# The end of a fused transformer block: score PSUM reopened as single banks, denominators turned by 32x32 transposes, late W1 groups through gelu from PSUM

## Chip, cores, metric

One NeuronCore of a Trainium2 chip. The metric is the device time of one execution, in microseconds (us). The times below are medians of runs in the fast state; no run used here was marked slow, and one (e10_turn_thrice) is a single run of unknown state, used only for its trace. Besides the whole time I use the **tail**: in one trace, the stretch from the end of the last exp (which is the start of the following `ACT_TABLE_LOAD` on ScalarE) to the end of the span. It turns out to repeat far better than the whole time does.

In the views of the profile, PE is TensorE, DVE is VectorE, ACT is ScalarE and POOL is GpSimd. The **granted clock** of a run is the mean share of its full clock that TensorE was given, as the profiler lists it.

## The reference

An adaLN-conditioned block: layer norm, attention with 32 heads of 16 (S = 2048, D = 512), residual, layer norm, a dense layer of 1376 with gelu, residual. All inputs are bf16.

```python
mod = (_silu(c) @ w_mod).reshape(c.shape[0], 6, 1, -1)
sa, ca, ga, sb, cb, gb = (mod[:, i].copy() for i in range(6))
h = _layernorm(x) * (1 + ca) + sa
x = x + ga * _A_ref(h, A_wqkv, A_wo)          # attention
h = _layernorm(x) * (1 + cb) + sb
x = x + gb * _B_ref(h, B_w1, B_b1, B_w2, B_b2)  # gelu(h @ w1 + b1) @ w2 + b2
```

## The kernel before

A small list scheduler inside the kernel places every operation. `op(engine, fn, us, deps, ...)` makes one, `acq=` takes a buffer from a pool (`Res`), `rel=` gives buffers back, and `gate=` holds an operation until a condition is true. TensorE computes scores, ScalarE takes exps of 1536 or 1024 columns from PSUM, VectorE does some of the exps in another way ("shifts"), TensorE multiplies by V with a column of ones (so row 16 of each 32 holds the denominator), and W1, W2 and Wo fill the gaps.

Queries come in four blocks of 512. For the last block all heads of the first 256 queries are done first, so that their dense layer (`block_tail(b, 2)`, here called the **older half**) can partly run under the exps. The last 256 queries are two tiles of 128, **tile 2** and **tile 3** (`last_half`). In the traces a table load of 1.28 us stands between the last exp and the first gelu (`ACT_TABLE_LOAD`), and the kernel holds back all gelus of both halves until the last exp is done.

```python
    SPAN = (3, 2)
    ...
    r_st = [res(f"st{n}", 1, [P, n * QB], FP32, pp) for n in SPAN]   # scores: one tile of 3 banks, one of 2
    r_od = res("od", 1, [P, QB], FP32, pp)                            # P @ V of the current heads
    r_ax = res("ax", 2, [P, QB], FP32, pp)                            # everything else
    ...
    # block_tail, the older half (part = nt < TPB)
        for f in range(NF):                                           # NF = 11 groups of W1
            mm = chain([(lambda ps, f=f, j=j: nc.tensor.matmul(
                out=ps[:, 0:N], lhsT=W1[:, j, f * P:(f + 1) * P], rhs=h.tile[:, j, 0:N],
                start=(j == 0), stop=(j == NC - 1)), nt * MM / NC) for j in range(NC)],
                hd + [o_late["w1"], g], kind, r_ax, (h,))
            ev.append(op("DVE", lambda o, f=f, mm=mm: nc.vector.tensor_scalar(      # add b1, to SBUF
                out=g.tile[:, f, 0:N], in0=mm.tile[:, 0:N], scalar1=b1c[:, f:f + 1], scalar2=None,
                op0=ALU.add), ...))
        if part:                                                      # three gelus in SBUF after the last exp
            ge = [op("ACT", ... Gelu_apprx_tanh ...,
                gate=lambda: units[0] == NR * NT * 4) for lo, hi in ((0, 4), (4, 8), (8, NF))]
    ...
    # last_half: tiles 2 and 3
        big = [take(x) for x in r_st]
        r_t = Res("t", sum(SPAN), lambda i: big[i >= SPAN[0]].tile[       # five slots in the two score tiles
            :, (i % SPAN[0]) * QB:(i % SPAN[0] + 1) * QB])
        acc = {t: take(r_t, big) for t in tiles}
        ...
        for n, t in enumerate(tiles):
            ml = []
            for p in range(2):
                cols = slice(p * HB + (t % 2) * P, p * HB + (t % 2 + 1) * P)
                sh = ... nc.vector.stream_shuffle(out=OD.tile[:, cols], in_=od.tile[:, cols], mask=[16] * 32)
                rc = ... nc.vector.reciprocal(out=OD.tile[:, cols], in_=OD.tile[:, cols])     # 128 columns
                ml.append(... nc.vector.tensor_tensor(out=OT.tile[:, cols], in0=od.tile[:, cols],
                                                      in1=OD.tile[:, cols], op=ALU.mult))
            ...   # 2 Wo matmuls (WoP), y = ps * ga, residual, statistics, rstd on GpSimd, z, 4 PE transposes,
            ...   # 2 modulations on VectorE and 2 on ScalarE
            for f in range(NF):                                       # 4 matmuls of 128 columns, then gelu from PSUM
                mm = op("PE", w1, 4 * 0.071, hd, lat=PEL, mode=full, kind="last", acq=r_t, prio=0.3)
                gd.append(op("ACT", ... Gelu_apprx_tanh, bias=b1c[:, f:f + 1] ..., (mm,), prio=0.3, rel=(mm,)))
            ...   # 12 matmuls of W2 (one is the bias row), y, residual, store
```

The softmax here doesn't subtract the row's maximum and nothing guards it: scores larger than these inputs give would overflow.

## Time and profile before

| | before |
|---|---|
| time, median (range), first 3 runs | 823.44 us (823.07 to 825.82) |
| span of the profiled run | 818.1 us |
| last exp's end | 784.05 us |
| tail | 34.05 us |
| first W1 matmul of tile 2 begins / last one ends, after the last exp's end | 10.5 / 16.1 us |
| last W1 matmul of tile 3 ends, after the last exp's end | 24.7 us |

The prediction below quotes the main lines and says how they are read. Here is one view more: ScalarE's timeline of tile 3 in the kernel before. Columns are start, duration of the row, engine, line, operation, output and input with sizes, count, and in brackets the idle time ahead of the row and what ended it.

```profile
804.00 0.81 ACT L1186 ACTIVATE g<-st,b1c 128x128 bf16<-128x128 f32 x2 [0.30 <-PE st L1183]
805.29 0.88 ACT L1186 ACTIVATE g<-st,b1c 128x128 bf16<-128x128 f32 x3 [0.47 <-PE st L1183]
806.61 0.37 ACT L1186 ACTIVATE g<-st,b1c 128x128 bf16<-128x128 f32 x1 [0.44 <-PE st L1183]
```

ScalarE does one to three gelus and then waits 0.3 to 0.5 us for TensorE. TensorE in turn waits for ScalarE, here in one row of its timeline and then in the summary of waits from 784 us on (engine, line, what it waited for: total us, times, longest):

```profile
804.87 0.61 PE L1183 MATMUL st<-blk,W 128*128 128x128 bf16 x8 [0.46 <-ACT g L1186]
```

```profile
ACT g L1186 <- PE st L1183: 4.1, 10, 0.9
PE st L1183 <- ACT g L1186: 3.7, 8, 1.0
```

### The profile page before, as it was taken

What the parts mean: (1) busy time and instruction counts of PE and PEld (TensorE: products, weight loads), DVE (VectorE), ACT (ScalarE), POOL (GpSimd) and SP (SyncE); (2) the same over time, 40 slices, a digit from 0 to 9 for tenths busy, and PEclk for the clock granted to TensorE, in tenths of its full rate; (3) what the DMA queues carried; (4) which work ended last, traced back from release to release, by engine and by line L of the source; (5) the groups of instructions that cost most, each with busy time, mean ns of one, the idle gap of its engine ahead of it and who ended that gap; (6) DMA issues with size and microseconds to landing.
All of it is one profiled execution on the core that took longest, in us unless ns stands there. A gap on an engine that the chain in (4) does not pass through costs nothing.

```text
span 818.1 us, 20211 instructions
## 1 busy us (share of the span) xinstructions
PE 754.6 (92%) x8236; PEld 281.0 (34%) x8236; DVE 740.1 (90%) x1296; ACT 768.8 (94%) x688; POOL 95.1 (12%) x238
## 2 busy tenths in 40 slices
PE   7889999999989999989999999999999899999996
PEld 3433333332223232222233233232233344434453
DVE  7728997989999999988999999888999999999992
ACT  2899999999999999989999999999999999999963
POOL 4321303100001100000000100000002100010010
PEclk9999999999999999979999999999999999999999
DMA  6304100102100000001100000010100001001110
GB/s 206 104 1 125 27 17 16 30 21 66 41 19 15 18 16 16 18 1 31 48 22 19 15 6 15 24 29 21 45 15 20 11 12 42 18 24 29 24 36 20
DMA packets 34199, 26.22 MB, mean 32 GB/s; under 512 B 15006, under 2 KB 29503, under 8 KB 34107
## 3 DMA queue, kind: packets, MB, share of 16 engines
q1 hardware_dynamic: 33578, 24.94, 10.8%
q8 instruction: 64, 1.05, 0.5%
q14 instruction: 29, 0.23, 0.1%
q10 hardware_dynamic: 528, 0.00, 0.0%
HBM read 21.30 MB, written 2.61 MB: 29 GB/s over the span
## 4 chain that ended last, share of the span: by engine, by line
ACT 39%; PE 28%; DVE 17%; issue 13%; DMA 2%; SPq 0%; ACTq 0%; DVEq 0%
ACT pt L797 37%; PE od L886 9%; PE st L748 8%; DVE ph L838 7%; DVE sh L853 6%; PE ax L1041 2%; PE ax L1072 2%; PE ax L748 2%; ACT g L1085 1%; DMA xb<-in_A_x_dram 1%; PE ax L643 1%; DVE g L1076 1%; DVE OD L911 1%; ACT blk L574 1%; PE st L1183 1%
## 5 line engine op out<-in xcount | busy, mean ns | idle before, releaser
L797 ACT ACTIVATE pt<-st 128x1536 bf16<-128x1536 f32 x635 | 724.3, 1289 | 11.6 <-PE st L748 9.2
L838 DVE TENSOR_SCALAR ph<-ax 128x512 int16<-128x512 f32 x460 | 299.1, 681 | 16.0 <-PE ax L748 13.7
L853 DVE TENSOR_SCALAR sh<-ph 128x2048 int16<-128x2048 int16 x460 | 299.3, 689 | 2.7 <-PE od L886 2.4
L748 PE MATMUL st<-qm,kT 32*128 32x512 bf16 x1588 | 249.8, 385 | 30.0 <-ACT pt L797 23.1
L748 PEld LDWEIGHTS <-kT 32*128 32x128 bf16 x2048 | 86.1, 91 | 257.1 <-issue 246.2
L886 PE MATMUL od<-sh,VX 128*32 128x512 bf16 (+1 forms) x2336 | 163.5, 340 | 5.9 <-DVE sh L853 4.8
L748 PE MATMUL ax<-qm,kT 32*128 32x512 bf16 x460 | 161.9, 382 | 6.6 <-DVE ph L838 4.7
L886 PE MATMUL od<-pt,VEB 128*32 128x512 bf16 (+1 forms) x1976 | 151.6, 343 | 0.9 <-ACT pt L797 0.4
L886 PEld LDWEIGHTS <-VEB 128*32 128x32 bf16 x2560 | 64.9, 96 | 77.2 <-issue 61.5
L886 PEld LDWEIGHTS <-VX 128*32 128x32 bf16 x2336 | 57.9, 95 | 81.9 <-issue 71.7
L938 POOL TENSOR_TENSOR OT<-OD,RB 128x256 bf16<-128x256 f32 x38 | 28.2, 752 | 332.6 <-DVE sh L853 239.3
L886 PE MATMUL od<-ph,VEB 128*32 128x512 bf16 (+1 forms) x584 | 46.6, 341 | 1.5 <-DVE OD L911 1.5
L1072 PE MATMUL ax<-blk,W 128*128 128x512 bf16 (+1 forms) x176 | 41.5, 354 | 0.9 <-DVE ph L838 0.4
L938 POOL TENSOR_TENSOR OS<-OD,RB 128x256 bf16<-128x256 f32 x24 | 17.3, 728 | 205.5 <-DVE sh L853 170.8
L643 PE MATMUL ax<-blk,w 128*128 128x512 bf16 x124 | 36.5, 382 | 2.9 <-ACT blk L574 1.6
L1041 PE MATMUL ax<-w,g 128*128 128x512 bf16 x112 | 31.9, 400 | 0.9 <-ACT g L1085 0.9
L684 POOL TENSOR_SCALAR VX<-VEB 128x128 bf16<-128x128 bf16 x64 | 22.8, 356 | 77.0 <-DVE VEB L584 73.3
L1076 DVE TENSOR_SCALAR g<-ax,b1c 128x512 bf16<-128x512 f32 (+1 forms) x44 | 29.5, 676 | 0.4 <-PE ax L1072 0.2
L911 DVE COPY OD<-od 128x512 f32<-128x512 f32 x31 | 21.1, 681 | 7.4 <-issue 6.3
L558 DVE BATCH_NORM_STATS2 ln_s<-xb 128x6 f32<-128x512 bf16 x32 | 21.6, 675 | 2.4 <-DMA xb<-in_A_x_dram 2.3
L1041 PEld LDWEIGHTS <-g 128*128 128x128 bf16 x176 | 14.4, 99 | 26.9 <-issue 15.0
L584 DVE CAST VEB<-ax 128x512 bf16<-128x512 f32 x15 | 10.2, 681 | 12.8 <-PE ax L668 12.8
(110 smaller groups left out, 382.1 us busy)
## 6 DMA issues: line engine op xcount, KB each, us to landing
RB<-rn SPq DMA_DIRECT2D x124, 64.0 KB
xb<-in_A_x_dram SPq DMA_DIRECT2D x8, 512.0 KB
out_dram<-o SPq DMA_DIRECT2D x16, 128.0 KB
w<-in_A_wqkv_dram SPq DMA_DIRECT2D x3, 512.0 KB
W<-in_B_w_dram SPq DMA_DIRECT2D x1, 1376.0 KB
blk<-in_w_mod_dram SPq DMA_DIRECT2D x2, 512.0 KB
g<-in_w_mod_dram SPq DMA_DIRECT2D x2, 512.0 KB
xb<-in_w_mod_dram SPq DMA_DIRECT2D x2, 512.0 KB
```

Of the source, the lines that this page charges most:

```text
L643: return chain([(lambda ps, j=j: nc.tensor.matmul(out=ps[:, 0:QB], lhsT=w.tile[:, j, cc * P:(cc + 1) * P], rhs=o_h[b].tile[:, j, :], start ...
L684: nc.gpsimd.tensor_scalar(out=v_cols(VX[(t, ph)])[:, 8 * cc:8 * cc + 8, 0:16], in0=v_cols(v_tile(t, 0))[:, 8 * cc:8 * cc + 8, 0:16], scala ...
L748: nc.tensor.matmul(out=o.tile[:, k * QB:(k + 1) * QB], lhsT=kT[cc][kb][rows, ko * P:(ko + 1) * P], rhs=qm.tile[rows, par, :] if hb is None ...
L797: nc.scalar.activation(out=e.tile[:, 0:len(got) * QB], in_=o.tile[:, 0:len(got) * QB], func=ACT.Exp, scale=ESC)
L838: nc.vector.tensor_scalar(out=ph.tile[:, o.row * QB:(o.row + 1) * QB], in0=o.tile, scalar1=PH_B, scalar2=0.0, op0=ALU.add, op1=ALU.max)
L853: sh = op("DVE", lambda o, j=j: nc.vector.tensor_scalar(out=o.tile, in0=first.tile, scalar1=PH_SH[j], scalar2=None, op0=ALU.add), 0.6, es, ...
L886: nc.tensor.matmul(out=o_od[r].tile[32 * i:32 * i + 32, n * HB:n * HB + w], lhsT=v_tile(kt, ph)[:, c0:c0 + 32], rhs=got[i][:, at:at + w], ...
L911: OD = op("DVE", lambda o: nc.vector.tensor_copy(out=o.tile, in_=od.tile), 0.6, (last,), prio=0.0, acq=r_OD, rel=(od,))
L938: two = [op("POOL", lambda o, c=c: after_dve(nc.gpsimd.tensor_tensor(out=OT.tile[:, c * HB:(c + 1) * HB], in0=OD.tile[:, c * HB:(c + 1) * HB],
L1041: nc.tensor.matmul(out=ps, lhsT=g[:, f, col:col + P], rhs=rhs, start=False, stop=(f == NF - 1))
L1072: mm = chain([(lambda ps, f=f, j=j: nc.tensor.matmul(out=ps[:, 0:N], lhsT=W1[:, j, f * P:(f + 1) * P], rhs=h.tile[:, j, 0:N], start=(j == ...
L1076: ev.append(op("DVE", lambda o, f=f, mm=mm: nc.vector.tensor_scalar(out=g.tile[:, f, 0:N], in0=mm.tile[:, 0:N], scalar1=b1c[:, f:f + 1], s ...
```

## The change

The intent is to shorten what follows the last exp, in three parts. **Banks**: the PSUM pool of the scores is closed after the last exp and reopened as five tiles of one bank, so that a wait on one group is no longer a wait on its neighbours. **Turns**: the denominators are brought to eight columns by a 32x32 transpose, divided there, and transposed back, in place of a shuffle and a reciprocal over 128 columns. **Direct**: of the older half, W1 groups 4 to 10 wait for the last exp, go to the new banks, and are read by gelu straight from PSUM, bias included; VectorE's seven adds go.

```diff
+    PSUM_F = 4
-    r_st = [res(f"st{n}", 1, [P, n * QB], FP32, pp) for n in SPAN]
+    scores = ExitStack()
+    ps = scores.enter_context(tc.tile_pool(name="ps", bufs=1, space=psum))
+    r_st = [res(f"st{n}", 1, [P, n * QB], FP32, ps) for n in SPAN]
...
+    def bank(i):
+        if not banks:
+            scores.close()
+            pt = ctx.enter_context(tc.tile_pool(name="pt", bufs=1, space=psum))
+            banks.extend(pt.tile([P, QB], FP32, name=f"t{n}") for n in range(sum(SPAN)))
+        return banks[i]
+    r_t = Res("t", sum(SPAN), bank)
...
         for f in range(NF):
+            direct = part and f >= PSUM_F
             mm = chain([...
-                hd + [o_late["w1"], g], kind, r_ax, (h,))
+                hd + [o_late["w1"], g, over if direct else None], kind,
+                r_t if direct else r_ax, (h,))
+            if direct:
+                ev.append(op("ACT", lambda o, f=f, mm=mm: nc.scalar.activation(
+                    out=g.tile[:, f, 0:N], in_=mm.tile[:, 0:N], func=ACT.Gelu_apprx_tanh,
+                    bias=b1c[:, f:f + 1], scale=1.0), 0.36, (mm,), lat=0.15, prio=0.4, rel=(mm,)))
+                continue
...
-                gate=lambda: units[0] == NR * NT * 4) for lo, hi in ((0, 4), (4, 8), (8, NF))]
+                gate=finished) for lo, hi in ((0, 2), (2, PSUM_F))]
...
-                sh = ... stream_shuffle(out=OD.tile[:, cols], in_=od.tile[:, cols], mask=[16] * 32)
-                rc = ... reciprocal(out=OD.tile[:, cols], in_=OD.tile[:, cols])
-                ml.append(... tensor_tensor(out=OT.tile[:, cols], in0=od.tile[:, cols], in1=OD.tile[:, cols], op=ALU.mult))
+            sh = ... transpose(out=turned(0), in_=half(od.tile))
+            rc = ... reciprocal(out=den, in_=OD.tile[:, 16:HB:32])                       # 8 columns
+            bk = ... transpose(out=turned(1)..., in_=den.unsqueeze(2).to_broadcast([P, 8, 32]))
+            ml = [... tensor_tensor(out=half(OT.tile), in0=half(od.tile), in1=turned(1), op=ALU.mult)]
...
-                    o.ps = big[o.slot >= SPAN[0]].tile.bitcast(BF16)[:, c0:c0 + 2 * P]
+                    o.ps = o.tile.bitcast(BF16)[:, 0:2 * P]
```

More of the change, by code (lines that the diff above doesn't have):

```diff
@@ L1042, in w2_mm, with finished, open_banks, go @@
                              start=False, stop=(f == NF - 1))
+    def finished():
+        return units[0] == NR * NT * 4
+    banks = []
+    def bank(i):
[5 more added lines that the diff above has]
+    r_t = Res("t", sum(SPAN), bank)
+    r_t.free[:] = [1e18] * sum(SPAN)
+    def open_banks():
+        def go(o):
+            for n in range(sum(SPAN)):
+                r_t.free[n] = o.end
+        big = [op("POOL", None, 0.0, (), lat=0.0, prio=0.0, acq=x, gate=finished) for x in r_st]
+        op("POOL", go, 0.0, big, lat=0.0, prio=0.0)
     def block_tail(b, nt=TPB):
@@ L1070, in block_tail @@
         ev = []
+        over = op("POOL", None, 0.0, (), lat=0.0, prio=0.0, gate=finished) if part else None
+        if part:
+            open_banks()
         for f in range(NF):
+            direct = part and f >= PSUM_F
             mm = chain([(lambda ps, f=f, j=j: nc.tensor.matmul(
@@ L1093, in block_tail @@
                         for f in range(NF)], (prev, o_late["w2"]), "part" if part else kind, r_ax, (g,), 3,
-                       lambda f: ge[f // 4 if part else 0])
+                       lambda f: ge[0] if not part else ge[f >= 2] if f < PSUM_F else ev[f])
             prev = mm
@@ L1121, in last_half @@
         tiles = (2, 3)
-        big = [take(x) for x in r_st]
-        r_t = Res("t", sum(SPAN), lambda i: big[i >= SPAN[0]].tile[
-            :, (i % SPAN[0]) * QB:(i % SPAN[0] + 1) * QB])
-        acc = {t: take(r_t, big) for t in tiles}
+        acc = {t: take(r_t) for t in tiles}
         early = {t: op("PE", lambda o, t=t: wo_mm(acc[t].tile, b, t, 0, 3), 3 * MM,
@@ L1130, in last_half, with half, turned @@
         for n, t in enumerate(tiles):
-            ml = []
-            for p in range(2):
-                cols = slice(p * HB + (t % 2) * P, p * HB + (t % 2 + 1) * P)
-                sh = op("DVE", lambda o, cols=cols: nc.vector.stream_shuffle(
-                    out=OD.tile[:, cols], in_=od.tile[:, cols], mask=[16] * 32), 0.25,
-                    (o_last[r], OD, s), prio=0.06 + n)
-                rc = op("DVE", lambda o, cols=cols: nc.vector.reciprocal(
-                    out=OD.tile[:, cols], in_=OD.tile[:, cols]), 0.9, (sh,), prio=0.05 + n)
-                ml.append(op("DVE", lambda o, cols=cols: nc.vector.tensor_tensor(
-                    out=OT.tile[:, cols], in0=od.tile[:, cols], in1=OD.tile[:, cols], op=ALU.mult),
-                    0.25, (rc, OT), prio=0.04 + n))
+            den = work.tile([P, 8], FP32, name=f"den{t}")
+            def half(x, t=t):
+                return x.rearrange("p (a q) -> p a q", a=2)[:, :, (t % 2) * P:(t % 2 + 1) * P]
+            def turned(n):
+                return OD.tile[:, n * HB:(n + 1) * HB].rearrange("p (a q) -> p a q", a=2)
+            sh = op("DVE", lambda o, t=t, half=half: nc.vector.transpose(out=turned(0), in_=half(od.tile)), 0.35,
+                    (o_last[r], OD, s), prio=0.06 + n)
+            rc = op("DVE", lambda o, den=den: nc.vector.reciprocal(
+                out=den, in_=OD.tile[:, 16:HB:32]), 0.12, (sh,), prio=0.05 + n)
+            bk = op("DVE", lambda o, den=den: nc.vector.transpose(
+                out=turned(1).rearrange("p a q -> p (a q)"),
+                in_=den.unsqueeze(2).to_broadcast([P, 8, 32])), 0.35, (rc,), prio=0.045 + n)
+            ml = [op("DVE", lambda o, t=t, half=half: nc.vector.tensor_tensor(
+                out=half(OT.tile), in0=half(od.tile), in1=turned(1), op=ALU.mult),
+                0.36, (bk, OT), prio=0.04 + n)]
             def wo2(o, t=t):
@@ L1167, in tr @@
                 def tr(o, t=t, js=js):
-                    c0 = (o.slot % SPAN[0]) * 2 * QB
-                    o.ps = big[o.slot >= SPAN[0]].tile.bitcast(BF16)[:, c0:c0 + 2 * P]
+                    o.ps = o.tile.bitcast(BF16)[:, 0:2 * P]
                     for n, j in enumerate(js):
```

## The prediction

> **What bounds the kernel now.** I read the page first, then the table of busy time by stretch, then the timeline of each engine and the chain that ended last for the final 40 us, then the waits there. The page says that ScalarE's exps set the pace of nearly the whole span: 635 of them fill 724 us and have 11.6 us of idle time before them.
>
> ```profile
> span 818.1 us, 20211 instructions
> L797 ACT ACTIVATE pt<-st 128x1536 bf16<-128x1536 f32 x635 | 724.3, 1289 | 11.6 <-PE st L748 9.2
> ```
>
> The change leaves that part alone. The built kernels show it: on ScalarE and VectorE the order of instructions is the same up to the last exp and the last of the shifts before the last PV matmuls; on TensorE the first difference is some ten microseconds before that, where two groups of W1 matmuls are taken out. So the question is the tail: from the last exp's end at 784.05 to the span's end at 818.1 lie 34.05 us, and only there can time move. By stretch (columns: length, then busy time and instruction counts of each engine, clock):
>
> ```profile
> 784.00:790.00 6.00, 5.27 (x52) 2.98 (x43) 6.00 (x18) 3.42 (x4) 0.00 (x0) 1.00 0.16 55
> 790.00:795.00 5.00, 4.90 (x28) 2.08 (x28) 4.97 (x16) 1.68 (x4) 0.79 (x2) 1.00 0.00 0
> 795.00:800.00 5.00, 3.15 (x42) 2.53 (x40) 2.84 (x7) 3.09 (x10) 0.80 (x2) 1.00 0.09 30
> 800.00:805.00 5.00, 3.87 (x32) 2.13 (x30) 0.69 (x2) 2.02 (x5) 0.00 (x0) 1.00 0.00 0
> 805.00:810.00 5.00, 3.28 (x37) 2.10 (x36) 0.70 (x2) 2.75 (x9) 0.00 (x0) 1.00 0.00 0
> ```
>
> The tail has two regimes. Up to 795 VectorE is full (6.00 of 6.00, 4.97 of 5.00). From 795 to 810 nobody is: TensorE 10.3 of 15 us, ScalarE 7.9. VectorE's full stretch holds the denominators of the last heads (shuffle, reciprocal, multiply, twice for each token tile) and seven bias adds of W1:
>
> ```profile
> 785.26 0.29 DVE L1134 STREAM_SHUFFLE OD<-od 128x128 f32<-128x128 f32 x1
> 785.46 1.75 DVE L1137 RECIPROCAL OD<-OD 128x128 f32<-128x128 f32 x2
> 787.13 0.41 DVE L1140 TENSOR_TENSOR OT<-od,OD 128x128 bf16<-128x128 f32 x2
> 787.47 0.86 DVE L1076 TENSOR_SCALAR g<-ax,b1c 128x256 bf16<-128x256 f32 x2
> 788.25 0.67 DVE L1151 TENSOR_TENSOR y<-st,ga_bc 128x512 bf16<-128x512 f32 x1
> ```
>
> The later regime is a ping-pong, in the chain that ended last: one or two groups of W1, then gelu, then W1 again; and then a block of W2 that nothing hides.
>
> ```profile
> 805.29 0.63 ACT g L1186 x2
> 805.92 0.04 issue
> 805.96 0.62 PE st L1183 x8
> 806.58 0.02 issue
> 806.61 0.38 ACT g L1186
> 806.98 0.04 issue
> 807.02 0.40 PE st L1183 x4
> ...
> 809.81 2.48 PE st L1041 x11
> 812.29 1.31 PE ax L1041 x6
> ```
>
> Five banks of scores are free by then, but they are two tiles, one of three banks and one of two. A matmul into one bank of a tile waits for the gelu that reads another bank of it: the waits list TensorE's W1 behind gelu for 3.7 us and gelu behind W1 for 4.1 us, and the second tile's PSUM transposes cost the same sort of alternation (802.0 to 803.7, VectorE, ScalarE, VectorE, ScalarE in turn).
>
> [...] The 128x128 f32 shuffle here took 294 ns; a 128x256 transpose is then about 0.43 us (estimate; no transpose on VectorE is in this trace). [...] reciprocal [...] 128x128 took 0.938 us, 128x16 took 0.241, 128x4 took 0.178; 128x8 is about 0.20.
>
> **The change, part by part.** Times below continue the trace of before, so that 784.05 is still the last exp. Paces from rows of the trace: a 512-column matmul every 0.217 us (eight in 1.90, the first 0.38), a 256-column one 0.112, a 128-column one 0.056, each 0.17 more until its result is seen; gelu 128x128 0.367 alone and 0.25 apart in a row, hence 128x256 about 0.47 and 0.36; a hand-over 0.03.
>
> Denominators. Removed on the path for the first tile: the shuffles at 785.04 to the multiplies' end at 787.54, then two bias adds, so that y began at 788.25. Added: the last PV matmul ends near 784.8, transpose 0.43, reciprocal 0.20, transpose 0.43, one multiply over 256 columns 0.41, four hand-overs 0.12: 786.4. TensorE reaches the two Wo matmuls by then (six early Wo 1.3 from 784.7, five W1 of 256 columns 0.56: 786.6), 0.43 and 0.17: y begins at about 787.2, 1.05 us earlier. From y on the durations stay: y 0.69, add 0.42, statistics 0.69 and 0.18, GpSimd 0.97, z 0.41, with hand-overs 3.5: z at 790.7.
>
> W1 from PSUM. Seven bias adds (7 x 0.466 = 3.3 us of VectorE) and three large gelus (1.06, 1.06, 0.84) go; two 128x512 gelus of about 0.62 and seven 128x256 at 0.36 come, 3.6 us on ScalarE in place of 3.0, but beside other work. Seven groups of four 256-column matmuls, two of them formerly under the exps, take TensorE from 786.0 to about 789.6 with the two Wo matmuls. Then eight of the W2 matmuls (0.31 for the bias row and six at 0.217, two more later) fill its time: the transposes start at 791.2, where z no longer holds them; they started at 792.82.
>
> Token tile 2. Transposes 0.23, ScalarE's two modulations end at about 792.4, W1 begins 792.4 (before: 794.55). Now five groups are in flight, so the eleven gelus run 0.25 apart: first at 792.8, last ends 795.7; before, 794.97 to 800.56. Between the modulations TensorE also does the second tile's Wo matmuls, so its y begins near 792.0, where it began at 795.62. That is the largest single step: 3.6 us, of which the old wait in front of those matmuls (OT of tile 3 and the shared score tile) is all.
>
> Token tile 3. The same 3.5 us from y to z: 795.5. W1 of tile 2 is done at 794.9, bias row and one W2 by 795.4, so transposes at 795.5 (before 801.49). Each half now has its own bank: ScalarE done at 796.8 (before 803.71). Eleven gelus on four banks, 0.25 apart: 797.2 to 800.1, TensorE's last W1 at 799.3. Here 9.3 us are won in all, the last W1 matmuls being at 808.6 before and at 799.3 now.
>
> The block at the end. Some is given back. In the built order 20 matmuls of 512 columns followed the last W1 group before (2, 12, 6). Now it is 6, 12, 3 and 12, so 33, because the second W2 group of the older half is put last. Two are bias rows: 31 x 0.217 + 2 x 0.31 = 7.3 us, from 799.3 to 806.6, and 0.17 more. Before, it ended at 813.6. So 2.5 us of the 9.3 go back, 6.8 remain. After that y 0.69, add 0.42 and hand-overs bring 808.0, against 814.77, and the output transfer with the end takes the same 3.3 us. Sum: 811.3 in place of 818.1, 6.8 us less. A second count agrees: all of TensorE's work from 784.7 is 54 matmuls of 512 columns (11.7), four bias rows (1.2), 28 of 256 (3.1) and 96 of 128 (5.4): 21.4 us, to 806.1 if it never waited. It would be all but saturated, so a longer transpose or gelu gains or loses little, and there is nothing more to win without less matmul work.
>
> **The rivals.** First, TensorE's order binds: it takes its queue in order, and one late z or OT stalls everything behind. For it: slacks are only 0.3 to 0.5 us at both transposes. Each of four such points could cost 0.3 to 0.5, and the gain falls to about 5 us: 818.5. Against it: the W2 pieces are placed exactly there. Second, the 32x32 transposes from PSUM, or with a repeated source, run at half the rate: 0.53 us more on the first tile, partly under W1: 817.3. Third, reopening the score banks adds a wait for all exps, or the five banks still depend on each other. Against: in the built kernel each W1 group waits for the one earlier reader of its bank. If it were so, the tail keeps the ping-pong of 9 us and the W2 surplus remains: about 824. Fourth, the whole 34 us are 4% of the span, so even a perfect tail cannot reach 2% (16.5 us): TensorE's 21.4 us stand against it.
>
> **Range and chances.** The worked gain is 6.8 us; I take 6.5, since small hand-overs tend to be missed and not overcounted: 823.44 - 6.5 = 816.9. The low end 815.0 is a gain of 8.4, with W2 a little faster and noise of a run; the high end 819.2 has the first rival in full and 0.7 us of run spread (823.07 to 825.82 before). A change over 2% either way has about one chance in a hundred each.
>
> **What would show it.** Last exp unchanged near 784; transposes of about 0.43 us and a reciprocal of about 0.2; second y 3.5 us earlier; gelus 0.25 us apart in rows of eleven, TensorE's waits on gelu nearly gone; 33 unbroken W2 matmuls of some 7.3 us at the end; TensorE over 95% busy from 785 to 807. Wrong would be: gaps of 0.4 us between gelus, a TensorE wait over 0.5 us at transposes, or a different time of the last exp.

Some of these figures, with what the traces show beside them:

- A transpose of 128x256 at 0.43 us was an estimate of mine: 0.294 us of the 128x128 shuffle and 0.133 us for 128 columns more. VectorE's f32 copies in the trace of before give that for 128 columns (166 ns for 8 columns at L546, 691 and 684 for 512 at L1022: 1.035 ns a column), but no trace then showed that a transpose keeps this pace. The four of the changed kernel took 417 to 452 ns. The second rival's 0.53 us is 512 columns at 1.035 ns more each.
- The reciprocals of 128, 16 and 4 columns, 0.938, 0.241 and 0.178 us, lie 6.2 ns a column apart from 16 to 128 and 5.3 from 4 to 16. Eight columns took 0.204 us in the changed kernel.
- The 128x256 gelu at 0.47 alone and 0.36 apart is an estimate too: in the trace of before gelus of 1024 and 768 columns took 1.057 and 0.843 us, so 0.107 for 128 columns. In the changed kernel one took 0.475 us, and the row of six took 2.66 us, 0.437 apart, near the 0.45 of the four W1 matmuls (0.112 each) that feed one.
- That TensorE takes its queue in order, as the first rival has it, shows in e10_turn_thrice: it stood 0.35 us for z with two matmuls later in its queue whose inputs were ready.

## The result and the profile after

The changed kernel took 815.74 us (median of 4 runs, 811.54 to 818.25), the kernel before 823.26 us in 4 runs. The ratio is 0.990 (95% interval 0.985 to 0.995): "same" by the 2% rule, and inside the predicted range. A ratio here and below is the mean time of one kernel's fast runs over the mean of the other's fast runs of the same rounds, so it is not quite the ratio of the medians.

The page of the changed kernel, in its lines for the span and the exps:

```profile
span 809.7 us, 20210 instructions
L800 ACT ACTIVATE pt<-st 128x1536 bf16<-128x1536 f32 x635 | 723.9, 1286 | 10.1 <-PE st L751 6.7
```

The exps are unchanged. ScalarE's timeline shows where the tail starts and how the gelus of tiles 2 and 3 run now:

```profile
782.08 1.28 ACT L1114 ACT_TABLE_LOAD   x1
...
790.92 2.95 ACT L1222 ACTIVATE g<-t,b1c 128x128 bf16<-128x128 f32 x11 [0.30 <-PE t L1219]
...
795.39 2.95 ACT L1222 ACTIVATE g<-t,b1c 128x128 bf16<-128x128 f32 x11 [0.30 <-PE t L1219]
```

Eleven gelus are one row, (2.95 - 0.37) / 10 = 0.258 us apart. The tail is 809.7 - 782.08 = 27.62 us, 6.43 less than before. The other 1.97 us of this profile's gain lie ahead of the last exp; the experiments show them to be run noise. VectorE, with both y rows that mark when a tile's layer norm can begin:

```profile
783.02 0.45 DVE L1169 STREAM_TRANSPOSE OD<-od 128x256 f32<-128x256 f32 x1 [0.56 <-issue]
783.51 0.20 DVE L1171 RECIPROCAL den<-OD 128x8 f32<-128x8 f32 x1
783.75 0.45 DVE L1173 STREAM_TRANSPOSE OD<-den 128x256 f32<-128x256 f32 x1
784.23 0.42 DVE L1176 TENSOR_TENSOR OT<-od,OD 128x256 bf16<-128x256 f32 x1
...
790.28 0.68 DVE L1188 TENSOR_TENSOR y<-t,ga_bc 128x512 bf16<-128x512 f32 x1
```

And the stretches that answer to those of before (length, then busy time of TensorE, its weight loads, VectorE, ScalarE, GpSimd; last the clock, the DMA share and GB/s):

```profile
782.00:787.00 5.00, 5.00 (x54) 3.40 (x54) 3.41 (x8) 4.30 (x9) 0.00 (x0) 1.00 0.22 74
787.00:792.00 5.00, 5.00 (x50) 3.33 (x48) 4.42 (x12) 3.23 (x11) 0.80 (x2) 1.00 0.00 2
792.00:797.00 5.00, 4.91 (x65) 3.81 (x63) 1.34 (x5) 4.29 (x17) 0.80 (x2) 1.00 0.01 3
797.00:802.00 5.00, 5.00 (x32) 2.45 (x30) 1.17 (x3) 1.34 (x6) 0.00 (x0) 1.00 0.08 26
```

TensorE, which had 10.3 of 15 us between 795 and 810, is now busy in 19.91 of 20 us. All 44 W1 matmuls of a tile are one row of its timeline:

```profile
790.47 2.65 PE L1219 MATMUL t<-blk,W 128*128 128x128 bf16 x44
...
794.94 2.80 PE L1219 MATMUL t<-blk,W 128*128 128x128 bf16 x44
```

The tail ends with W2, from 797.58 to 805.28. "Busy" counts a matmul until its result is seen, so short pauses between matmuls don't show (each of a row of 128-column ones is listed with 0.218 us, and they come 0.057 apart): by the paces of the prediction the same work adds up to 21.4 us, and it took 22.4 (from 782.85 to 805.28).

### The profile page after: what moved, and what is told of

It is laid out like the page before. It is cut to its first block, busy times and chain, and to the rows that moved or that the text cites. A ratio compares the mean times of both kernels' runs of the same rounds, so it can differ in the third digit from the quotient of the medians.

```text
span 809.7 us, 20210 instructions
## 1 busy us (share of the span) xinstructions
PE 751.2 (93%) x8236; PEld 280.0 (35%) x8236; DVE 735.9 (91%) x1281; ACT 768.6 (95%) x694; POOL 95.4 (12%) x238
## 4 chain that ended last, share of the span: by engine, by line
ACT 39%; PE 27%; DVE 16%; issue 14%; DMA 2%; SPq 1%; POOL 0%; POOLq 0%; DVEq 0%; ACTq 0%
ACT pt L800 37%; PE od L889 9%; PE st L751 8%; DVE ph L841 7%; DVE sh L856 6%; PE ax L1044 2%; PE ax L751 2%; PE ax L1100 2%; DMA xb<-in_A_x_dram 1%; PE ax L646 1%; ACT g L1119 1%; DVE g L1110 1%; DVE OD L914 1%; PE t L1044 1%; PE ax L1036 1%
## 5 line engine op out<-in xcount | busy, mean ns | idle before, releaser
L800 ACT ACTIVATE pt<-st 128x1536 bf16<-128x1536 f32 x635 | 723.9, 1286 | 10.1 <-PE st L751 6.7
L751 PE MATMUL st<-qm,kT 32*128 32x512 bf16 x1588 | 250.2, 385 | 29.5 <-ACT pt L800 22.7
L1100 PE MATMUL ax<-blk,W 128*128 128x512 bf16 (+1 forms) x148 | 37.8, 370 | 0.6 <-DVE ph L841 0.4
L1110 DVE TENSOR_SCALAR g<-ax,b1c 128x512 bf16<-128x512 f32 (+1 forms) x37 | 26.5, 719 | 0.4 <-PE ax L1100 0.2
L587 DVE CAST VEB<-ax 128x512 bf16<-128x512 f32 x15 | 10.3, 683 | 12.8 <-PE ax L671 12.8
```

What stands on the lines that cost most here:

```text
L751: nc.tensor.matmul(out=o.tile[:, k * QB:(k + 1) * QB], lhsT=kT[cc][kb][rows, ko * P:(ko + 1) * P], rhs=qm.tile[rows, par, :] if hb is None ...
L800: nc.scalar.activation(out=e.tile[:, 0:len(got) * QB], in_=o.tile[:, 0:len(got) * QB], func=ACT.Exp, scale=ESC)
L1100: mm = chain([(lambda ps, f=f, j=j: nc.tensor.matmul(out=ps[:, 0:N], lhsT=W1[:, j, f * P:(f + 1) * P], rhs=h.tile[:, j, 0:N], start=(j == ...
```

## The experiments

All gave right results. Tails are read from each run's own trace. "Equal clock" is a fit of mine over the 151 fast runs of the jobs below and the first four of the changed kernel: one level for each kernel and one common slope of the span on the run's mean granted TensorE clock (0.969 to 0.992). The slope is -0.42 us for each 0.001 of clock, and the scatter about it 1.2 us (within one kernel and without the slope it is 2.0).

| kernel | time, median | ratio to before (95%) | tail | tail against 34.05 | span at equal clock against before (95%) |
|---|---|---|---|---|---|
| changed (first runs; e6_after) | 815.74; 815.40 | 0.990 (0.985-0.995); 0.990 (0.988-0.993) | 27.62; 27.68 | -6.4 | -6.4 ± 0.8 |
| e1_banks: banks | 815.12 | 0.992 (0.989-0.994) | 27.80 | -6.25 | -5.6 ± 0.8 |
| e2_turns: turns | 821.82 | 1.000 (0.998-1.001) | 34.52 | +0.5 | +0.3 ± 0.7 |
| e3_no_turns: banks, direct | 814.62 | 0.991 (0.988-0.994) | 27.63 | -6.4 | -6.5 ± 0.9 |
| e4_no_direct: banks, turns | 816.45 | 0.994 (0.991-0.996) | 28.57 | -5.5 | -5.2 ± 0.8 |
| e5_before: the kernel before | 822.21 | 1.000 (0.998-1.002) | 34.06 | 0.0 | |
| e7_banks3: three banks | 814.57 | 0.990 (0.987-0.993) | 28.00 | -6.05 | -6.6 ± 1.0 |
| e8_psumf6; e11_psumf6_again | 816.42; 813.96 | 0.991 (0.988-0.994); 0.991 (0.989-0.993) | 26.69; 26.60 | -7.4 | -7.3 ± 0.7 |
| e9_psumf6_no_turns | 814.47 | 0.992 (0.989-0.994) | 26.82 | -7.2 | -7.3 ± 1.0 |
| e10_turn_thrice (one run) | 815.00 | | 28.22 | -5.8 | |

My theory (A) was that the shared score tiles made the ping-pong, and that once it is gone TensorE's total work sets the length of the tail. Its rivals: (B) VectorE, full for the first 11 us, was what held the tail, so denominators and bias adds carry the gain; (C) three parts of about equal worth.

### e1_banks: the five banks alone

```diff
 (changed kernel)
-            direct = part and f >= PSUM_F
+            direct = False          # and the three SBUF gelus, the shuffle and the long reciprocal of before
```

> The five one-bank score tiles alone; denominators by shuffle and reciprocal and the seven bias adds on VectorE as before. Measure: the tail, from the end of the last exp to the end of the span (34.05 us before, 27.62 after). Theory A (the shared score tiles made the ping-pong; once that is gone TensorE's work sets the end): tile 2 starts as before, but its eleven gelus run 0.25 us apart, the Wo matmuls of tile 3 no longer wait behind them, z of tile 3 comes near 15 us after the last exp, and only 20 W2 matmuls follow the last W1: tail 27.4 to 28.4, nearly the whole gain. Theory B (VectorE, full until 795, was what held the tail, so denominators and bias adds carry the gain): at most 3 us are won, tail 31 or more. Theory C (three parts of about 2 us each): tail near 32.

Tail 27.80, as A says: 6.25 of the 6.43 us come from the storage of five PSUM groups alone. In its ScalarE timeline:

```profile
785.50 1.28 ACT L1114 ACT_TABLE_LOAD   x1
...
801.98 2.94 ACT L1216 ACTIVATE g<-t,b1c 128x128 bf16<-128x128 f32 x11 [0.31 <-PE t L1213]
```

The eleven gelus of tile 3 are one row, though denominators and bias adds are those of before. But y of tile 3 starts at

```profile
796.87 0.69 DVE L1182 TENSOR_TENSOR y<-t,ga_bc 128x512 bf16<-128x512 f32 x1
```

which is 11.37 us after the last exp's end. Before it was 11.57, in the changed kernel it is 8.20. So the banks hardly move that y, and still win the tail. The rows of TensorE's timeline come in the same order as in the kernel before, a few missing records aside; what the banks took away is waiting. In the first 20 us after the last exp TensorE is busy for 18.86 us, against 16.65 before; the transposes of tile 3 start 14.94 us after the last exp's end in place of 17.44, and its W1 is done at 18.7 in place of 24.5.

This tail isn't yet full, though: TensorE has 0.9 us less to do here than in the changed kernel (two W1 groups run under the exps), and stands twice near the start, 0.35 us for the denominators and 0.34 us for a bias add.

### e2_turns: the transposes alone

```diff
 (kernel before)
-            shuffle, reciprocal over 128 columns, multiply, twice a tile
+            transpose, reciprocal over 8 columns, transpose, multiply
```

> The 32x32 transposes alone, on the two old score tiles. Theory A: y of tile 2 comes about 0.8 us earlier and the second Wo matmuls 1.5 to 2 us earlier, but the gelu ping-pong of tiles 2 and 3 stays, and the scheduler now leaves 30 W2 matmuls for after the last W1 where it left 20: tail 33.5 to 34.8, no gain. Theory B: tail 31 or less. Theory C: tail near 32.

Tail 34.52: no gain, a half microsecond lost, as A says. The y of tile 3 begins 9.96 us after the last exp's end, 1.6 us earlier than before, and the time goes again: TensorE still stops for readers of the shared tile, once for y itself:

```profile
796.79 0.83 PE L1189 MATMUL st<-blk,W 128*128 128x128 bf16 x12 [0.78 <-DVE y L1157]
```

and 30 matmuls of W2 remain after the last W1 where 20 did (by the built order; 29 of the 30 are in the trace). B and C fall with e1 and e2.

### e3_no_turns: the changed kernel with the old denominators

```diff
 (changed kernel)
-            transpose, reciprocal over 8 columns, transpose, multiply
+            shuffle, reciprocal over 128 columns, multiply, twice a tile
```

> The changed kernel with the old denominators (banks and late gelu from PSUM stay). Theory A: TensorE is so nearly full that W2 and W1 matmuls fill the time in which VectorE divides; tail 27.3 to 28.3, within 0.7 us of the changed kernel. Theory B: the reciprocals (3.6 us of VectorE) come back onto the path, tail 29.5 or more. Theory C: tail near 29.7.

Tail 27.63 against 27.62: nothing lost. The y of tile 3 is again at 11.37 us after the last exp's end, 3.2 us later than in the changed kernel, and it doesn't matter. While VectorE divides, TensorE does W1 and W2 of the older half; what it has done by then it need not do at the end (18 matmuls of W2 after the last W1, where the changed kernel has 33).

### e4_no_direct: the changed kernel with the old bias adds

```diff
 (changed kernel)
-            direct = part and f >= PSUM_F
+            direct = False          # and the three SBUF gelus of before
```

> The changed kernel with the old bias adds on VectorE and three gelus in SBUF (banks and transposes stay). Two W1 groups (0.9 us of TensorE) then run under the exps again. Theory A: tail 26.8 to 27.7, the same as or a little shorter than the changed kernel, since TensorE has 0.9 us less to do there while VectorE's adds lie beside it. Theory B: 3.3 us of bias adds come back onto VectorE, tail 29 or more. Theory C: tail near 29.7.

Tail 28.57, 0.95 us longer than the changed kernel and outside what A expected; B and C expected more still. The TensorE timeline shows what I missed:

```profile
791.42 1.32 PE L1100 MATMUL ax<-blk,W 128*128 128x256 bf16 x8 [0.70 <-DVE g L1110]
793.33 0.37 PE L1041 MATMUL ax<-b_row,ones_row 1*128 1x512 bf16 x1 [0.59 <-DVE g L1110]
```

On the two `ax` tiles, W1 of the older half goes at the pace of VectorE's adds, some of which queue between y, residual and statistics of tile 2: four of the seven come after y, where in e1_banks three do. TensorE stands 1.3 us for them (in e1_banks 0.34 for an add and 0.35 for the denominators), more than the 0.9 us of work that it has less. So the direct gelus are worth about 0.95 us beside banks and turns, but only 0.17 us beside banks alone (27.80 to 27.63), where the scheduler put all of W2 of one older tile ahead. The same four kernels read the other way say what the transposes are worth: beside banks and adds they lengthen the tail by 0.77 us (27.80 to 28.57), as they did by 0.47 alone in e2_turns; beside banks and direct gelus they change nothing.

### e5_before and e6_after: both kernels once more

No edit.

> The kernel before, unchanged, as a second trace. Its tail (last exp's end to the end of the span) should be 34.05 us again to within 0.3 us, while the last exp's end itself may lie anywhere between 782 and 787 us, as it did in the six traces so far. If so, the part of the changed kernel's first trace that was won ahead of the last exp (2.0 us) is run noise and no effect of the change. If instead it ends near 784.0 again and the changed kernel near 782.1 again, there is an effect ahead of the tail that I have not explained.

> The changed kernel, unchanged, as a second trace and for a tighter interval of its time. Tail 27.62 to within 0.3 us; the last exp's end between 782 and 787. Ratio of times 0.990 to 0.9935 (6.4 us of 822).

Tails 34.06 and 27.68, within 0.06 us of the first traces. The last exp ended at 786.34 and 784.92 us here, at 784.05 and 782.08 in the first traces. Over all the profiled runs it lies between 782 and 789.5 us, so what was won ahead of the tail in the first profile is noise of the runs. Over the 13 traces it comes earlier, on the whole, at a higher granted clock: e8_psumf6, whose last exp ended at 789.51, had a mean granted clock of 0.974, the first trace of the changed kernel 0.987. The ratio of times, 0.990, is in the expected range.

### e7_banks3: three banks in place of five

```diff
-    r_t = Res("t", sum(SPAN), bank)
+    r_t = Res("t", 3, bank)       # likewise in the two loops over its slots
```

> The changed kernel with three of the five one-bank tiles in use. A bank comes round in a W1 group (0.23), its 0.17 of latency, a gelu (0.37) and two hand-overs (0.07): 0.84 us, so gelus can follow each other every 0.25 us with four banks and every 0.28 with three; in tile 3 the open W2 sum holds one of the three, which leaves two and 0.42. Theory A (the rotation, so the number of free banks, is what the change bought; TensorE fills part of the gaps with W2): tail 28.2 to 29.5. Rival (it is enough that tiles are separate, two would do, or the order of TensorE's queue does it all): tail 27.3 to 27.9.

Tail 28.00, between the two expectations, so neither is confirmed. The gelus of tile 3 do come in pairs, 0.88 us a pair:

```profile
804.34 0.62 ACT L1222 ACTIVATE g<-t,b1c 128x128 bf16<-128x128 f32 x2 [0.25 <-PE t L1219]
805.22 0.63 ACT L1222 ACTIVATE g<-t,b1c 128x128 bf16<-128x128 f32 x2 [0.25 <-PE t L1219]
```

That is the slow rotation I expected, but TensorE fills each gap with W2 matmuls, so only 19 of them follow the last W1. Fewer banks cost 0.4 us as long as there is other work for the queue. My 0.42 us a gelu nearly held (0.44), as did my 0.28 with three banks (the eleven of tile 2 took 3.14 us, 0.277 apart); my cost of it did not. So 6.05 of the 6.43 us come with three separate tiles already.

### e8_psumf6 and e11_psumf6_again: two W1 groups under the exps again

```diff
-    PSUM_F = 4
+    PSUM_F = 6
```

> The changed kernel with PSUM_F = 6 in place of 4: two W1 groups of the older half run under the exps again, as in the kernel before, and seven gelus become five. If TensorE's work sets the length of the tail, as the trace of the changed kernel says (5.00 busy of 5.00 us in three of four stretches), 8 matmuls of 256 columns (0.9 us) go from it and the W2 block after the last W1 shrinks from 33 to 26 matmuls: tail 26.3 to 27.0. If the chain of layer norm and gelus sets it instead, nothing is won, since the two bias adds lie ahead of the first transpose (0.25 us later): tail 27.6 to 27.9.

> The version with PSUM_F = 6 once more, for its time: tail 26.69 to within 0.1 us; at the same granted clock 0.9 us faster than the changed kernel, which the spread of the runs (1.5 to 2.5 us) can hide: ratio to the kernel before 0.988 to 0.992.

Tails 26.69 and 26.60: 0.9 to 1.0 us shorter than the changed kernel. In e8_psumf6 the span is 816.2 us and the tail starts at

```profile
789.51 1.28 ACT L1114 ACT_TABLE_LOAD   x1
```

Eight matmuls of 256 columns are 8 x 0.112 = 0.9 us of TensorE. This is the direct test of A: take TensorE work out of the tail and the tail gets shorter by as much, although y of tile 3 starts half a microsecond later (8.70 us after the last exp's end against 8.20). In time, at equal clock, it is 0.9 ± 1.0 us ahead of the changed kernel: the tail is shown to be shorter. A faster whole is likely and not shown, since the two groups now run under the exps, and what they cost there is lost in the spread of the last exp's end.

### e9_psumf6_no_turns: the same with the old denominators

```diff
 (e8_psumf6)
-            transpose, reciprocal over 8 columns, transpose, multiply
+            shuffle, reciprocal over 128 columns, multiply, twice a tile
```

> PSUM_F = 6 with the old denominators (shuffle, 128-column reciprocal). Two of three tests of the transposes showed no gain from them while TensorE was the limit; here TensorE has 0.9 us less to do, so if they are ever worth something in this tail it should show. Theory A (TensorE's work sets the tail as long as any W2 is left to fill the waits): the Wo matmuls of both tiles and z come 1.3 us and more later, but the scheduler leaves only 12 W2 matmuls for the end: tail 26.3 to 27.2, within 0.5 us of the 26.69 with transposes. Rival (with less TensorE work the chain through the denominators is the limit): tail 27.8 or more.

Tail 26.82, 0.1 to 0.2 us longer than with transposes, and within A's range. It may be a first small gain from them, but the two traces with transposes differ by 0.09 us themselves, and here there is one.

### e10_turn_thrice: more VectorE work

```diff
-            sh = op("DVE", ... nc.vector.transpose(out=turned(0), in_=half(od.tile)), 0.35,
+            sh = op("DVE", ... [nc.vector.transpose(...) for _ in range(1 if t == 2 else 3)], 0.35,
```

> The changed kernel with the first transpose of tile 3's denominators done three times in place of once, the same result: 0.8 us more of VectorE, same order on TensorE. In the trace of the changed kernel z of tile 2 is ready 0.35 us before TensorE reaches its transposes and OT of tile 3 about 0.25 us before its Wo matmuls, so 0.8 us more should leave a wait of 0.45 to 0.6 us on TensorE, and tail 28.0 to 28.3: VectorE's chain then is hidden only up to that slack. If VectorE had far more slack than that, tail 27.6 to 27.8; if it were the limit itself, 28.4 or more.

Tail 28.22, in the expected range. The three transposes took 1.39 us in place of 0.42, so VectorE had 0.97 us more to do, not 0.8. VectorE's chain is hidden only up to its slack; beyond it TensorE waits at the transposes of tile 2, which start 7.80 us after the last exp's end in place of 7.30:

```profile
792.78 0.40 PE L1208 MATMUL t<-ident,z 128*128 128x128 bf16 x4 [0.35 <-DVE z L572]
```

The order of the queue was fixed at build for a shorter chain, and TensorE stood although two W2 matmuls of the older half, whose gelus had ended at 791.2, came later in it. In e3 and e9 the scheduler knew the longer durations, and their traces have all 12 W2 matmuls of the first older tile ahead of those transposes; that, and not idle VectorE, is my reading of why old denominators cost nothing there.

## Why the prediction was right, point by point

All times in us after the last exp's end (784.05 before, 782.08 after; the prediction's clock minus 784.05).

| step | before | predicted | measured |
|---|---|---|---|
| y of tile 2 begins | 4.20 | 3.15 | 3.34 |
| PE transposes of tile 2 begin | 8.77 | 7.15 | 7.30 |
| y of tile 3 begins | 11.57 | 7.95 | 8.20 |
| last gelu of tile 2 ends | 16.51 | 11.65 | 11.79 |
| PE transposes of tile 3 begin | 17.44 | 11.45 | 11.77 |
| W1 is done, W2 begins | 24.5 | 15.25 | 15.5 |
| last W2 matmul ends | 29.5 | 22.7 | 23.2 |
| end of the span (tail) | 34.05 | 27.25 | 27.62 |

- **The bound and its place**: right. The exps did not change (724.3 and 723.9 us) and all the gain lies in the tail. One sign of being wrong that the prediction names did appear, a different time of the last exp (782.08); e5 and e6 put it down to the runs.
- **Durations of the new operations**: right. Transposes 0.42 to 0.45 us (0.43 estimated), reciprocal of eight columns 0.204 (0.20), gelus 0.258 apart (0.25).
- **The block at the end**: 33 matmuls of W2 as read from the built order; 7.7 us where 7.3 and 0.17 were worked out (so not unbroken), with pauses of some 0.1 us between the sums.
- **TensorE nearly saturated**: right, 19.91 of 20 us, and e8 and e11 show that its work sets the length. The 21.4 us of work took 22.4, with pauses between matmuls that the count left out.
- **Size**: the tail's gain of 6.43 us fits the 6.5 on record. The medians, 815.74 and 815.40, are 1.2 and 1.5 us below the 816.9 predicted; the mean granted clock was 0.982 in the runs of the changed kernel and 0.980 in those of the kernel before, which at 0.42 us for each 0.001 is some 0.8 us of it, and the rest is within the scatter.
- **A slip in a sum**: two gelus at 0.62 and seven at 0.36 are 3.76 us, not 3.6; nothing rests on it.
- **What was wrong, though the sum was right**: the prediction calls the earlier y of tile 3 "the largest single step: 3.6 us". The y did come 3.4 us earlier, but with banks alone and in e3 it stays at 11.37 and the tail is the same. It also credits the denominators with the first microsecond; e3 shows that they are worth nothing in this kernel. And "the old wait in front of those matmuls (OT of tile 3 and the shared score tile) is all": e1 removes the shared tile and moves y by 0.2 us, so that part of the wait was OT. I had followed one chain and added up its steps; the second count, by TensorE's work, was the one that explains the size. That the steps came out within 0.5 us each says that the chain was followed rightly, not that each step was worth what it was credited with.
- **Rivals**: the first (TensorE's order binds, gain about 5 us) and the second (transposes at half rate) did not happen: the transposes took 417 to 452 ns, not the 0.7 us (0.43 and half of 0.53) that half the rate would make; e10 shows that the first is real once VectorE has 0.97 us more to do, and e4 when bias adds come late. Of the third, no TensorE group of the tail waits for a gelu any more. The fourth holds: the gain is 1%.

What stays open: how much of e4's 0.95 us is the adds' duration and how much the order in which the scheduler put them; no kernel here separates the two. That the same seven adds cost only 0.17 us between e1 and e3 speaks for the order.

## What to carry to other kernels

When a drain phase alternates between two engines, look first at what storage ties their groups together: five independent PSUM tiles in the place of two gave 6.25 of 6.43 us, without a single instruction made cheaper; with three in place of five, all three parts together still gave 6.05. Once the busiest engine of such a phase is full, moving a step of the other engines earlier was worth nothing here, even by 3.2 us (e3), and work taken out of the phase counted (0.9 us of matmuls, 0.9 us of tail), provided that the full engine wasn't made to wait instead (e4: 0.9 us less work, 0.95 us more tail). Compare a phase by its own length in the traces (0.1 us from run to run here) and not by the whole time (a standard deviation of 1.6 to 2.4 us in the runs of one kernel).

## What the traces and runs showed of the hardware

- TensorE, matmuls in a row: 44 of 128 columns took 2.65 us, the first 0.218: 56.5 ns each; eight of 512 took 1.90, the first 0.38: 217 ns.
- VectorE, 32x32 transposes of 128x256 f32: 417 to 452 ns from PSUM and 445 ns from a source repeated 32 times, near the 430 ns that the prediction estimated.
- VectorE, reciprocal of f32: 0.938 us for 128 columns and 0.241 for 16 are 6.2 ns a column; eight took 0.204.
- The span of this kernel, which ScalarE's exps pace, was about 0.42 us longer for each 0.001 less of TensorE's granted clock, which was most of the spread of the runs (2.0 us, 1.2 without it). Why it is so was not tested.
